# Splitting the first weight load of a decode kernel into four strided loads

## The chip, the cores and the metric

The kernel runs on one core of one Trainium2 chip. The metric is the device time of one execution in microseconds (us), of which the median over several runs is taken. The kernel before takes 692.08 us (three runs, 692.03 to 692.16). A share of 0.2% of that is 1.38 us.

## What is computed

One decode step of a gated mix of attention and a feed-forward block, for one token, all in float32. Cut to what matters:

```python
# x: 1x1x512; k_cache, v_cache: 1x8x32768x128; wq: 512x4096; wo: 4096x512
# w1, w3: 512x1792; w2: 1792x512; gate_w: 512
g = sigmoid((x * gate_w).sum(-1, keepdims=True))
q = (x @ wq).reshape(1, 1, 32, 128).transpose(0, 2, 1, 3)
k, v = repeat(k_cache, 4, axis=1), repeat(v_cache, 4, axis=1)   # 32 query heads on 8 kv heads
p = softmax(einsum("bhqd,bhkd->bhqk", q, k) * 128 ** -0.5)
a = einsum("bhqk,bhkd->bhqd", p, v).transpose(0, 2, 1, 3).reshape(1, 1, 4096) @ wo
b = (silu(x @ w1) * (x @ w3)) @ w2
out = g * a + (1 - g) * b
```

Every weight and every cache row is read once: 296 MB, nearly all of it the two caches (8 heads, 16.8 MB of keys and 16.8 MB of values for each).

## The kernel before, in words

Three regions of SBUF of 128 partitions x 64 KB each (`ra`, `rb`, `rc`) take all the large loads in turn. All of them are issued by SyncE (SP), in an order that the code writes out by hand.

The first three loads stand in `tile_gated_mix_decode_kernel`, ahead of the rest of the program: `wq` into `rc` (line 34 of the loop, semaphore `l_q`), then `w1` and `w3` into the two parts of `rb` (`l_w1`, `l_w3`). `wq` is viewed as 128 rows of 64 KB, one for each partition: four rows of the weight matrix lie in one partition. A jump (L38) with a barrier of all engines follows, since the first part of the program is closed there, and `_program` begins.

In `_program` SP issues the two halves of the first head's first key region (L131, L132, into `ra`), and then every further load waits for the region that it overwrites: `rb` for the feed-forward matmuls (L134, count `c_e`), `ra` and `rb` for the score matmuls (L138, L145, count `c_k`), `rc` for the copies of the query and then for the value matmuls (L143, L147). ScalarE (ACT) issues three small transfers: `x` (L168), `gate_w` (L169) and a row of zeros to the output (L175).

TensorE (PE) turns `x` onto the partitions (L200), makes the sum of the gate (L209), waits for `wq` (L210) and multiplies it (L215, 64 matmul records), then takes `w1` and `w3` (L242). VectorE (DVE) transposes the query rows (L227), ScalarE copies them into place (L231), and the loop over the eight heads starts: VectorE transposes the keys in 32x32 blocks (L355), TensorE makes scores (L284) and multiplies the values of the head before (L298), ScalarE makes the exponentials (L399). After the last head come the output projection with `wo` (L434) and the second feed-forward matrix `w2`, in five pieces (L441, L451).

Of the kernel before, what the change touches and what calls it, by code (L numbers as in the profile page):

```python
# [9 lines left out]
P = 128  # L10
# [14 lines left out]
@with_exitstack  # L25
def kernel(ctx, tc, x, k_cache, v_cache, wq, wo, w1, w3, w2, gate_w, out):
    nc = tc.nc
    rb, rc = (nc.alloc_sbuf_tensor(n, [P, 16384], F32).ap() for n in ("rb", "rc"))
    l_q, l_w1, l_w3 = (nc.alloc_semaphore(n) for n in ("l_q", "l_w1", "l_w3"))
    loads = [(rc, wq, l_q)]  # L30
    n = w1.shape[0] * w1.shape[1] // P
    loads += [(rb[:, i * n:(i + 1) * n], w, sem) for i, (w, sem) in enumerate(((w1, l_w1), (w3, l_w3)))]
    for to, w, sem in loads:
        i = nc.sync.dma_start(to, w.rearrange("(p c) n -> p (c n)", p=P)).then_inc(sem, 16)

        tc.no_tile_sem_insts.add(i.ins.name)
    tc.close()
    tc.compile()  # L38
    _program(nc, rb, rc, l_q, l_w1, l_w3, x, k_cache, v_cache, wq, wo, w1, w3, w2, gate_w, out)


def _program(nc, rb, rc, l_q, l_w1, l_w3, x, k_cache, v_cache, wq, wo, w1, w3, w2, gate_w, out):
    pe, dve, act, pool, sp = nc.tensor, nc.vector, nc.scalar, nc.gpsimd, nc.sync
# [163 lines left out]
    dve.tensor_copy(xp[:, :, 0], mc[:, NC:2 * NC]).then_inc(t_x, 1)  # L207
    take(t_x, 2)
    n_gate = c_q.by(pe.matmul(mc[:, 0:1], ones[0:1], gsm[0:1], start=True, stop=True))  # L209
    pe.wait_ge(l_q, 16)  # L210
    for c in range(NC):
        for b in range(2):
            for j in range(4):
# [225 lines left out]
    for k in range(W2[1]):  # L439
        t = k % 4  # L440
        i = pe.matmul(  # L441
            acc[32 * t:32 * t + 32, :], htp[:, k, :], w2t[:, k, :], start=False, stop=(k >= W2[1] - 4),
            skip_group_check=True,
        )
# [65 lines left out]
```

## Time and profile before

| what | value |
|---|---|
| median of three runs | 692.08 us |
| span of the profiled execution, first to last instruction | 690.5 us |
| what lies around the span, by the median | 1.6 us |
| busy: TensorE, VectorE, ScalarE, GpSimd | 55%, 44%, 6%, 1% of the span |
| mean granted TensorE clock | 0.763 of full speed |
| read from HBM | 296.23 MB, 429 GB/s over the span |
| packets on SP's queue | 6192, 99.3% of 16 DMA engines' span |

How to read it: the share of a compute engine says how long it worked, not whether anybody waited for it. The DMA share is the mean over the core's 16 DMA engines of the time in which a packet of theirs was on its way, so 1.00 is all 16 engines busy all of the time. In a table by windows, the bytes and the time of a packet are counted in the window in which it starts. So in a window shorter than a packet the share can lie far above 1, and such rows tell how many packets started: a packet of `wq` is one row of 65,536 bytes. Packets on SP's queue can be counted from the program: 5504 rows, and for each of the 43 transfers one small packet on each of 16 engines, together 6192.

### The profile page before, as it was taken

Reading aid. Unit: us, or ns where it says so; the run is one execution under the profiler, and the core shown is the slowest. Engines: PE = TensorE matmul, PEld = TensorE weight load, DVE = VectorE, ACT = ScalarE, POOL = GpSimd, SP = SyncE. Lnnn points to the kernel's source line nnn. Section 1 sums busy time; section 2 is a strip of 40 time slices with the busy share of each in tenths; the row PEclk is TensorE's granted clock in tenths of the full one; section 3 lists DMA queues with packets and bytes.
Section 4 is the critical chain, followed back from the end, with each engine's and each line's share of the span. In section 5 each row is a group of like instructions: output and inputs, shape, how many; then the busy total and the mean of one; then the engine's idle time right before and its main releaser. Section 6 shows DMA issues by size and latency. Waiting matters only on the chain. (4 is left out here: it accounts for less than half of the span.)

```text
span 690.5 us, 6710 instructions
## 1 busy us (share of the span) xinstructions
PE 380.2 (55%) x2946; PEld 107.8 (16%) x2946; DVE 307.0 (44%) x194; ACT 41.7 (6%) x111; POOL 7.1 (1%) x41
## 2 busy tenths in 40 slices
PE   1737256466463744567563735457463734466567
PEld 1200011103010121103020211103010211103122
DVE  1019378291725537091725447091815446191000
ACT  0020011002000010002000010002000010002000
POOL 0000000000000000000000000000000000000000
PEclk9975587879685876768577967778676966768678
DMA  9999999999999999999999999999999999999997
GB/s 410 400 434 455 425 430 430 448 440 429 426 429 437 425 437 444 437 429 425 433 433 433 444 440 429 425 429 437 429 444 440 433 425 429 437 425 437 441 417 318
DMA packets 6222, 296.35 MB, mean 429 GB/s; under 512 B 707, under 2 KB 963, under 8 KB 1094
## 3 DMA queue, kind: packets, MB, share of 16 engines
q1 hardware_dynamic: 6192, 296.23, 99.3%
q8 instruction: 6, 0.10, 0.1%
q14 instruction: 2, 0.02, 0.0%
q10 hardware_dynamic: 22, 0.01, 0.0%
HBM read 296.23 MB, written 0.00 MB: 429 GB/s over the span
## 5 line engine op out<-in xcount | busy, mean ns | idle before, releaser
L355 DVE STREAM_TRANSPOSE rb<-rb 128x2048 f32<-128x2048 f32 x64 | 141.8, 2274 | 150.3 <-DVEq L125 150.3
L284 PE MATMUL psum<-rb,winbuf 128*32 128x512 f32 x512 | 96.7, 836 | 122.9 <-PEq L125 122.9
L355 DVE STREAM_TRANSPOSE ra<-ra 128x2048 f32<-128x2048 f32 x64 | 141.4, 2276 | 43.0 <-DVEq L125 43.0
L298 PE MATMUL psum<-rc,prob 128*32 128x512 f32 x896 | 112.8, 660 | 41.3 <-PEq L125 41.3
L284 PE MATMUL psum<-ra,winbuf 128*32 128x512 f32 x512 | 87.5, 782 | 83.8 <-PEq L125 83.8
L298 PEld LDWEIGHTS psum<-rc,prob 128*32 128x32 f32 x896 | 33.6, 121 | 117.0 <-issue 116.8
L379 DVE TENSOR_REDUCE mx<-psum 128x4 f32<-128x1024 f32 x8 | 9.8, 1225 | 82.7 <-DVEq L125 82.7
L284 PEld LDWEIGHTS psum<-rb,winbuf 128*32 128x32 f32 x512 | 13.5, 125 | 202.7 <-issue 202.7
L393 ACT COPY sbuf<-psum 128x512 f32<-128x512 f32 x16 | 9.9, 618 | 478.0 <-PE psum L284 478.0
L284 PEld LDWEIGHTS psum<-ra,winbuf 128*32 128x32 f32 x512 | 14.9, 122 | 149.3 <-issue 149.3
L399 ACT ACTIVATE prob<-psum,nm 128x256 f32<-128x256 f32 x32 | 18.9, 695 | 39.3 <-DVE nm L387 39.3
L308 PE MATMUL psum<-ident,sbuf 128*64 128x64 f32 x512 | 16.7, 223 | 0.8 <-PEq L125 0.8
L308 PEld LDWEIGHTS psum<-ident,sbuf 128*64 128x64 f32 x512 | 15.6, 138 | 7.6 <-issue 7.6
L360 DVE SCALAR_TENSOR_TENSOR otall<-psum,gate,recip 128x4 f32 (+1 forms) x8 | 1.7, 214 | 32.8 <-DVEq L125 32.8
L298 PE MATMUL psum<-rb,prob 128*32 128x512 f32 x64 | 8.5, 690 | 9.7 <-DMA rb<-in_A_v_cache_dram 9.7
L215 PE MATMUL psum<-rc,xp 128*32 128x512 f32 x64 | 9.8, 782 | 4.7 <-DMA rc<-in_A_wq_dram 4.7
L434 PE MATMUL psum<-rc,oq 128*32 128x512 f32 x64 | 10.7, 829 | 2.6 <-DMA rc<-in_A_wo_dram 2.2
L271 POOL COPY winbuf<-winraw 32x16 f32<-32x16 f32 x32 | 6.1, 191 | 535.4 <-PE psum L284 499.7
L242 PE MATMUL psum<-rb,xp 128*32 128x448 f32 x64 | 8.6, 690 | 5.4 <-DMA rb<-in_B_w_dram 5.4
L298 PE MATMUL psum<-ra,prob 128*32 128x512 f32 x64 | 9.6, 770 | 3.3 <-DMA ra<-in_A_v_cache_dram 3.3
L200 PE MATMUL psum<-ones,ob 1*128 1x1 f32 x8 | 2.0, 370 | 15.2 <-DMA prob<-in_gate_w_dram 15.2
L318 PE MATMUL psum<-fold,ob 128*128 128x4 f32 x64 | 8.4, 255 | 0.8 <-PEq L125 0.8
(62 smaller groups left out, 79.0 us busy)
## 6 DMA issues: line engine op xcount, KB each, us to landing
ra<-in_A_k_cache_dram SPq DMA_DIRECT2D x2, 4096.0 KB, 52.6
rc<-in_A_wo_dram SPq DMA_DIRECT2D x2, 4096.0 KB, 45.5
rb<-in_B_w_dram SPq DMA_DIRECT2D x2, 3584.0 KB, 34.7
ra<-in_B_w_dram SPq DMA_DIRECT2D x1, 1792.0 KB, 33.4
ra<-in_B_w_dram SPq DMA_DIRECT2D x1, 1024.0 KB, 35.5
ra<-in_B_w_dram SPq DMA_DIRECT2D x1, 512.0 KB, 36.3
ra<-in_B_w_dram SPq DMA_DIRECT2D x2, 128.0 KB, 36.0
rc<-in_A_v_cache_dram SPq DMA_DIRECT2D x14, 30.4
```

The source lines that it names most:

```text
L215: m = pe.matmul(pq[b][32 * j:32 * j + 32, :], xp[:, c, :], rc[:, o:o + REP * DH], start=(c == 0), stop=(c == NC - 1),)
L242: i = pe.matmul(ps[32 * j:32 * j + 32, 0:FJ], xp[:, c, :], rb[:, o:o + FJ], start=(c == 0), stop=(c == NC - 1))
L271: pool.tensor_copy(winbuf[32 * r:32 * r + 32, 16:144].rearrange("p (c k) -> p c k", k=32)[:, :, 4 * r:4 * r + REP], winraw[32 * r:32 * r + ...
L284: i = pe.matmul(s_ps[m][32 * g:32 * g + 32, :], winbuf[:, w:w + 32], region.rearrange("p (n c i) -> p c n i", c=4, i=32)[:, c, n:n + 16], ...
L298: i = pe.matmul(o_ps[32 * t:32 * t + 32, :], prob[:, w:w + 32], region[:, n * DH:(n + 4) * DH], start=(r == 0 and g == 0 and f == 0), stop ...
L308: i = pe.matmul(pf[64 * s:64 * s + 64, 64 * a:64 * a + 64], sbuf[:, a].rearrange("p i m -> p (i m)"), ident.rearrange("p (gf r s q) -> p s ...
L318: i = pe.matmul(mb[:, 0:REP], ob[:, b * P:(b + 1) * P], fold[:, 4 * b:4 * b + 4], start=(b == 0), stop=(b == 3))
L355: dve.transpose(part[:, c], part[:, c]).then_inc(t_tr, 1)
L379: dve.tensor_reduce(mx, pf.rearrange("p (a q) -> p q a", q=REP), axis=AX.X, op=ALU.max).then_inc(t_mx, 1)
L393: act.copy(sbuf[:, :, :, m], s_ps[m].rearrange("p (n i) -> p n i", i=32)).then_inc(t_ev, 1)
L399: act.activation(prob[:, 0:1024].rearrange("p (a n q) -> p n a q", a=16, q=REP)[:, :, :, q], pf.rearrange("p (n a q) -> p n a q", n=16, q= ...
L434: pe.matmul(acc[32 * t:32 * t + 32, :], oq[:, k:k + 32], rc[:, k * D:(k + 1) * D], start=(k < 4), stop=False, skip_group_check=True,)
```

## The change

The one load of `wq` becomes four loads into the same places, each of some of the partitions: every eighth from 0 (16 rows), every eighth from 4 (16 rows), every fourth from 2 (32 rows), every second from 1 (64 rows). Together they are the 128 rows. All four raise `l_q` by 16, and TensorE waits for 64 in place of 16. Source rows go with the partitions, so each partition holds what it held before.

```diff
-    loads = [(rc, wq, l_q)]
-    n = w1.shape[0] * w1.shape[1] // P
-    loads += [(rb[:, i * n:(i + 1) * n], w, sem) for i, (w, sem) in enumerate(((w1, l_w1), (w3, l_w3)))]
+    wqd, w1d, w3d = (w.rearrange("(p c) n -> p (c n)", p=P) for w in (wq, w1, w3))
+    n = w1d.shape[1]
+    parts = [slice(first, P, step) for first, step in ((0, 8), (4, 8), (2, 4), (1, 2))]
+    loads = [(rc[s], wqd[s], l_q) for s in parts]
+    loads += [(rb[:, 0:n], w1d, l_w1), (rb[:, n:2 * n], w3d, l_w3)]
     for to, w, sem in loads:
-        i = nc.sync.dma_start(to, w.rearrange("(p c) n -> p (c n)", p=P)).then_inc(sem, 16)
+        i = nc.sync.dma_start(to, w).then_inc(sem, 16)
...
-    pe.wait_ge(l_q, 16)
+    pe.wait_ge(l_q, 64)
```

The only engine whose list of instructions changes is SP, at its start. Before, SP's first instructions are these (destination, source, partitions x elements, and in brackets the semaphore that one waits for; "in_B_w" is `w1`, `w3` or `w2`):

```order
L505 UNCONDITIONAL_BRANCH [waits barrier_Pool_Activation_PE_DVE_SP_release]
L34 DMA rc<-in_A_wq_dram 128x16384
L34 DMA rb<-in_B_w_dram 128x7168 x2
L38 UNCONDITIONAL_BRANCH
L131 DMA ra<-in_A_k_cache_dram 128x8192 [waits barrier_Pool_Activation_PE_DVE_SP_release]
L132 DMA ra<-in_A_k_cache_dram 128x8192
L134 DMA rb<-in_A_k_cache_dram 128x16384 [waits c_e]
```

After the change, the same place reads (line numbers are higher by two):

```order
L507 UNCONDITIONAL_BRANCH [waits barrier_Pool_Activation_PE_DVE_SP_release]
L36 DMA rc<-in_A_wq_dram 16x16384 x2
L36 DMA rc<-in_A_wq_dram 32x16384
L36 DMA rc<-in_A_wq_dram 64x16384
L36 DMA rb<-in_B_w_dram 128x7168 x2
L40 UNCONDITIONAL_BRANCH
L133 DMA ra<-in_A_k_cache_dram 128x8192 [waits barrier_Pool_Activation_PE_DVE_SP_release]
L134 DMA ra<-in_A_k_cache_dram 128x8192
L136 DMA rb<-in_A_k_cache_dram 128x16384 [waits c_e]
```

Three more transfers stand ahead of `w1` and `w3`, ahead of the barrier behind the jump (L38, now L40), and so ahead of the first keys; nothing else has moved, on SP or elsewhere.

## The prediction

> **What bounds the kernel now.** I read the page first, then stretches of the span, then the first microseconds.
>
> ```profile
> DMA  9999999999999999999999999999999999999997
> q1 hardware_dynamic: 6192, 296.23, 99.3%
> 22.50:342.50 320.00, 180.25 (x1354) 46.79 (x1354) 164.12 (x97) 21.86 (x61) 3.82 (x20) 0.75 1.00 434
> 342.50:662.50 320.00, 175.20 (x1378) 50.67 (x1382) 138.79 (x85) 16.73 (x44) 2.29 (x12) 0.75 1.00 433
> ```
>
> The page's DMA digits never fall from the first slice to the last but one, and SP's queue fills 99.3% of 16 engines' span. The last two columns of the windows are DMA share and GB/s: 1.00 and 434, then 1.00 and 433, over 640 us in which keys, values, VectorE's share and the clock's ups and downs all differ. The kernel is bound by its transfers, and they run against one flat ceiling. From the queue's row one engine moves 296.23 MB / (16 x 0.993 x 690.5 us) = 27.0 GB/s, so one row of `wq`, 65,536 bytes, takes 2.42 us, and the 8 rows that each engine has of `wq` 19.4 us.
>
> So whatever `wq` gains or loses at the front moves all that stands behind it, unless a cover exists. I looked for one in SP's own waits and in how long the first keys take:
>
> ```profile
> SPq L147 <- PE psum L298: 264.5, 7, 40.5
> SPq L134 <- PE psum L242: 42.8, 1, 42.8
> 3.22 0.43 SPq L132 DMA_DIRECT2D ra<-in_A_k_cache_dram  x1
> 46.50 0.33 SPq L134 DMA_DIRECT2D rb<-in_A_k_cache_dram  x1
> DMA to landing us min/median/max: 57.2/57.2/57.2
> rc<-in_A_v_cache_dram SPq DMA_DIRECT2D x14, 30.4
> ```
>
> SP does wait for buffers, but always with work queued. The second half of the first keys (issued at 3.22, the fifth row is its time to landing) lands at 60.4 us, while the next load is issued at 46.5 us: 14 us of queue are left. In the heads a value load takes 30.4 us from issue to landing, of which its own 128 rows need 19.4: 11 us of queue stand ahead. The engines are therefore never short of work, and both quantities shift with `wq` alike. A delay or gain in front reaches the end one to one; there is no slack in which it could vanish, and none in which it is made up.
>
> The end also hangs on the transfers:
>
> ```profile
> 677.63 2.14 another core or an unknown queue
> 679.82 5.34 PE psum L434 x32
> ```
>
> The second piece is TensorE's work on the second half of `wo`, and the gap before it is the wait for that half to land.
>
> **What the change takes from the start.** Here a gain is possible. Windows of 0.1 us tell when the first rows start (16 engines, one row each; 655 GB/s in 0.1 us is one row, 3277 is five):
>
> ```profile
> 1.70:1.80 0.10, 0.00 (x0) 0.00 (x0) 0.00 (x0) 0.00 (x0) 0.00 (x0) 1.00 9.89 3277
> 3.00:3.10 0.10, 0.00 (x0) 0.00 (x0) 0.08 (x1) 0.00 (x0) 0.05 (x1) 1.00 1.52 655
> 4.70:4.80 0.10, 0.00 (x0) 0.00 (x0) 0.00 (x0) 0.10 (x1) 0.00 (x0) 1.00 1.51 655
> 5.50:5.60 0.10, 0.00 (x0) 0.00 (x0) 0.00 (x0) 0.10 (x1) 0.00 (x0) 1.00 1.51 655
> ```
>
> Five engines start their first row at 1.7 us and the last at 3.0. The second rows start between 4.7 and 5.5, so the early ones needed 3 us for the first row, the last 2.4. The last engine stays 0.8 us behind the first. If the engines start late because descriptors for 128 rows are written before the last engine gets its first one, then a first load of 16 rows, one for each engine, takes away up to 3.0 - 1.7 = 1.3 us, and 0.8 us if the first engine's second row is the best that all can have. If it is a cost of the first access itself, it takes nothing. I take -0.4, the middle of 0 and the observed 0.8, and keep 0 to -1.3.
>
> **What it adds in issues and packets.** Three more transfers are issued by SP:
>
> ```profile
> 0.73 0.37 SPq L34 DMA_DIRECT2D rc<-in_A_wq_dram  x1
> 1.16 0.90 SPq L34 DMA_DIRECT2D rb<-in_B_w_dram  x2
> 2.84 0.33 SPq L131 DMA_DIRECT2D ra<-in_A_k_cache_dram  x1
> 22.84 9.81 PE L215 MATMUL psum<-rc,xp 128*32 128x512 f32 x64 [4.68 <-DMA rc<-in_A_wq_dram]
> 15.23 2.02 PE L200 MATMUL psum<-ones,ob 1*128 1x1 f32 x8 [15.23 <-DMA prob<-in_gate_w_dram]
> 21.60:21.70 0.10, 0.00 (x0) 0.00 (x0) 0.00 (x0) 0.00 (x0) 0.00 (x0) 1.00 0.67 287
> 687.00:688.00 1.00, 1.00 (x41) 0.80 (x36) 0.00 (x0) 0.51 (x1) 0.00 (x0) 1.00 0.35 119
> 688.00:689.00 1.00, 0.90 (x28) 0.59 (x19) 0.24 (x1) 0.24 (x1) 0.00 (x0) 1.00 0.00 0
> ```
>
> At 0.43 to 0.45 us each they push `w1`, `w3`, the barrier and everything issued behind it by 1.3 us. For SP that is covered by the rows of `wq` already queued: the first row of `w1` starts at 21.6 us (287 GB/s in 0.1 us is its 28,672 bytes), and it would be issued at 2.5. The barrier also delays ScalarE's small loads of `x` and `gate_w`, for which TensorE waits until 15.23 us. Behind them stand the gate and `xp`, and then TensorE has 4.68 us to spare before `wq` lands. A shift of 1.3 us, or of one more row of 2.42 us if their packets slip behind one, stays inside. Were that cover gone, TensorE would start L215 later; that costs nothing either until the 14 us of queue at L134 are used up. Cost: 0.
>
> The 3 x 16 more small packets: the engines are idle for 0.7% of 690.5 us, 4.8 us, of which 1.7 lie before the first row and some 2.5 behind the last (the last two rows: none starts after 688). At most 0.6 us are left for 43 transfers, 0.014 each. Three more cost at most 0.05 us.
>
> **What it does to the rate of `wq`.** This is the large unknown. Every large load of before covers 128 neighbouring partitions in one instruction, so whichever engine serves which partition, the pairing has always been the same, and the ceiling of 434 belongs to that pairing. The four parts break it: at one time the 16 engines write 16 partitions that lie 8 apart (part 1), then 16 others (part 2), and in parts 3 and 4 each engine's rows lie 4 and 2 apart. Two readings of the ceiling exist, and no row separates them. If the limit sits in the engine, 8 rows cost 8 x 2.42 us in any order: extra 0. If it sits where the data enters SBUF, with as many entrances as engines, and rows 8 apart fall on half of the entrances, then two engines share one for each row: 4.84 us in place of 2.42, extra 2.42 for each of 8 rows, 19.4 us. Two engines that share an entrance run in step, since they started together and go through the same sequence, so they meet again at the next row. What they are apart at the start, up to 0.8 us by the rows above, is saved on every collision: one collision costs 2.42 us less that distance. But the last pair decides, and among 8 pairs some are closely in step; I take -0.3 for this, and keep 6 x 0.8 = 4.8 us (six rounds, since two neighbouring rows on one entrance save only once) as the bound.
>
> I take the upper end, 19.4. The ceiling is the same for keys and values, for first and last heads, for rows of 64, 32 and 28 KB: the reading side changes addresses and sizes all the time and the rate does not move. What never changes is the set of destination partitions. That leaves engine or entrance, and an entrance that is just as wide as an engine is the natural partner of a flat 27.0 GB/s for each.
>
> [...]
>
> **The sum.** -0.4 (start) + 0.05 (packets) + 19.4 (sharing) - 0.3 (pairs not quite in step) = +18.7 us. Span 690.5 + 18.7 = 709.2 us; with the 1.6 us around it, which the median of 692.08 has beside the span, 710.8 us. Its own range: at most 19.4 + 0.05, at least 19.4 - 4.8 - 1.3 = 13.3, so 705.4 to 711.5.
>
> **Rivals.**
> - *The engine is the limit.* For it: each engine moves 27.0 GB/s whatever it moves. Against it: nothing in this trace. Then only the start counts: 692.08 - 0.4 = 691.7, between 690.7 and 692.1. It decides if a row keeps 2.42 us when its partition is 8 away from its neighbour's. This ends not slower.
> - *Only parts 1 and 2 collide.* If the rows of parts 3 and 4 are dealt out so that an entrance gets one engine at a time, or the pairs fall out of step after the first collisions, two rows cost double: 2 x 2.42 - 0.4 = +4.4, or 696.5, and up to 705 if they fall out of step later.
> - *The split does not place rows as it says.* If engines are tied to partitions, part 1's 16 rows go to 8 engines with two rows each, part 2's to the other 8, and each engine still has 8 rows in all at full rate. The order changes, the sum of rows does not: 692.1, with the start unimproved.
>
> [...]
>
> **How the numbers follow.** Full collisions 0.50, partial 0.17, engine's limit 0.24, rows tied to engines 0.07, a start that gains over 1.38 us 0.02. A measurement of this kernel can tell about 0.2%, 1.38 us, from no change. Slower: 0.50 + 0.17 = 0.67; same: 0.24 + 0.07 = 0.31; faster: 0.02. Leaving out either side would leave out more than 2 in 10, so the range reaches from the engine's limit with a good part of the start's gain, 691.0, to full collisions without any relief, 711.5; the likeliest case's own range stands above.
>
> **What would show it.** In windows of the first 45 us the DMA rate would be near 217 GB/s until about 41 us and 434 behind it, and TensorE's L215 (then L217) would start near 41.5 in place of 22.84. From there every row of the timeline is that of before, 18 to 19 us later: SP's L134 issue near 65 us, and the wait for `wo` the same length. If L215 starts at 22.0 to 22.8, the engine is the limit. If it starts near 27, only two rows collided. If the second rows start at 4.2 us on all engines the start was a matter of descriptors; if the first rows take 3 us again it was not. The prediction is wrong also if the delay shows at L215 and not at the end: then a cover that I deny exists.

## The result, and the profile after

The kernel with the change takes 697.24 us (median of five runs, 697.14 to 697.45) against 692.03 us for the kernel before in the same session: ratio 1.0077, 95% interval 1.0066 to 1.0088, or +5.2 us. The direction was forecast, the size was not: +18.7 us was the forecast, and 697.24 lies 0.7 us above the rival in which only parts 1 and 2 collide.

The page after the change, for the lines shown of before (DMA digits; SP's queue with packets, MB and share):

```profile
span 695.7 us, 6713 instructions
DMA  9999999999999999999999999999999999999997
GB/s 275 418 421 450 427 426 462 426 422 433 426 445 441 426 426 433 437 448 426 426 433 437 448 426 426 433 426 452 433 422 430 430 445 441 426 426 433 434 423 321
q1 hardware_dynamic: 6240, 296.23, 99.3%
```

Before, the rates of the 40 slices were:

```profile
GB/s 410 400 434 455 425 430 430 448 440 429 426 429 437 425 437 444 437 429 425 433 433 433 444 440 429 425 429 437 429 444 440 433 425 429 437 425 437 441 417 318
```

The span grew by 5.2 us. The queue's share is still 99.3%, and the digits look as full as before: the engines count as busy while a row crawls (a share of 1.04 at 223 GB/s, below). Only the rate tells: 275 GB/s in the first of 40 slices in place of 410, and from the second on about what it was. The 48 more packets (6240 for 6192) are the three loads' own.

Windows of the changed kernel show row by row what happened (last two columns DMA share and GB/s; 16 rows of 65,536 bytes start in each of these stretches but the second: 1311 x 0.8, 953 x 1.1, 955 x 1.1, 1751 x 0.6 and 1501 x 0.7 are all 1.05 MB):

```profile
2.00:2.80 0.80, 0.00 (x0) 0.00 (x0) 0.00 (x0) 0.00 (x0) 0.00 (x0) 1.00 6.08 1311
4.00:6.50 2.50, 0.00 (x0) 0.00 (x0) 1.11 (x5) 0.00 (x0) 0.79 (x5) 1.00 0.00 0
6.50:7.60 1.10, 0.00 (x0) 0.00 (x0) 0.03 (x1) 0.68 (x1) 0.00 (x0) 1.00 4.47 953
11.40:12.50 1.10, 0.00 (x0) 0.00 (x0) 0.00 (x0) 0.00 (x0) 0.00 (x0) 1.00 2.65 955
14.60:15.20 0.60, 0.00 (x0) 0.00 (x0) 0.00 (x0) 0.00 (x0) 0.00 (x0) 1.00 4.07 1751
17.00:17.70 0.70, 0.00 (x0) 0.00 (x0) 0.00 (x0) 0.00 (x0) 0.00 (x0) 1.00 3.48 1501
```

The 16 rows of part 1 start between 2.0 and 2.8, those of part 2 between 6.5 and 7.6, the first 16 of part 3 between 11.4 and 12.5, and none between 4.0 and 6.5. Where 16 rows start in a stretch, its length times the DMA share is the mean time of a row: 0.8 x 6.08 = 4.86 us in part 1, 1.1 x 4.47 = 4.92 in part 2, then 2.92, 2.44 and 2.44. The kernel before, with the first two rounds of its `wq`:

```profile
1.70:3.10 1.40, 0.00 (x0) 0.00 (x0) 0.08 (x1) 0.00 (x0) 0.20 (x1) 1.00 2.15 749
4.70:5.60 0.90, 0.00 (x0) 0.00 (x0) 0.00 (x0) 0.90 (x1) 0.00 (x0) 1.00 2.69 1165
```

There the first row took 1.4 x 2.15 = 3.01 us and the second 0.9 x 2.69 = 2.42. In two longer stretches of the changed kernel (parts 1 and 2; parts 3 and 4) and in the two stretches of 320 us that were shown of before:

```profile
2.00:11.40 9.40, 0.00 (x0) 0.00 (x0) 1.14 (x5) 1.28 (x1) 0.79 (x5) 1.00 1.04 223
11.40:26.70 15.30, 2.58 (x10) 2.43 (x10) 1.67 (x4) 0.17 (x1) 0.00 (x0) 1.00 0.98 412
22.50:342.50 320.00, 169.57 (x1338) 46.51 (x1338) 158.90 (x94) 21.83 (x61) 3.79 (x20) 0.77 1.00 432
342.50:662.50 320.00, 174.74 (x1386) 50.48 (x1382) 143.98 (x87) 16.71 (x44) 2.27 (x12) 0.77 1.00 433
```

Half the rate (223 GB/s), with a DMA share of 1.04, for the two rounds of 16 rows; nearly the full rate (412) for the other six rounds; and behind that nothing differs (432 and 433 in place of 434 and 433).

The timeline after the change, and two other rows on SP (the first keys' landing time and its waits):

```profile
0.73 2.48 SPq L36 DMA_DIRECT2D rc<-in_A_wq_dram  x4
5.12 0.33 SPq L133 DMA_DIRECT2D ra<-in_A_k_cache_dram  x1
18.10 2.02 PE L202 MATMUL psum<-ones,ob 1*128 1x1 f32 x8 [18.10 <-DMA prob<-in_gate_w_dram]
27.81 9.50 PE L217 MATMUL psum<-rc,xp 128*32 128x512 f32 x64 [6.79 <-DMA rc<-in_A_wq_dram]
51.10 0.33 SPq L136 DMA_DIRECT2D rb<-in_A_k_cache_dram  x1
DMA to landing us min/median/max: 59.8/59.8/59.8
SPq L149 <- PE psum L300: 264.5, 7, 40.6
```

TensorE starts on `wq` at 27.81 in place of 22.84, +4.97 us. The second half of the first keys (issued at 5.5 us) lands at 65.3 in place of 60.4, +4.9, with the next load issued at 51.1: the 14 us of queue are still there, and SP's long wait at L149 is the 264.5 us that it was at L147. The delay arose in the first three rounds, which end near 15 us, and was carried to the end.

One sign of the prediction did not come: the wait for `wo` is gone. TensorE came to the output projection 6.7 us later (678.99 in place of 672.29) and did both halves in one go; why it came 1.5 us later than the transfers' shift no run shows. The chain that ended last now hangs on the pieces of `w2`, the last transfers of the kernel:

```profile
678.99 9.88 PE L436 MATMUL psum<-rc,oq 128*32 128x512 f32 x64 [0.37 <-PEq L127]
655.87 35.88 DMA ra<-in_B_w_dram
691.79 2.15 PE psum L453 x60
```

The end still waits for a transfer, so the delay reaches it all the same.

### The profile page after: what moved, and what is told of

It is laid out like the page before. It is cut to its first block, busy times and chain, and to the rows that moved or that the text cites. A ratio compares the mean times of both kernels' runs of the same rounds, so it can differ in the third digit from the quotient of the medians.

```text
span 695.7 us, 6713 instructions
## 1 busy us (share of the span) xinstructions
PE 372.4 (54%) x2946; PEld 108.1 (16%) x2946; DVE 307.0 (44%) x194; ACT 41.7 (6%) x111; POOL 7.1 (1%) x41
## 3 DMA queue, kind: packets, MB, share of 16 engines
q1 hardware_dynamic: 6240, 296.23, 99.3%
## 5 line engine op out<-in xcount | busy, mean ns | idle before, releaser
L286 PE MATMUL psum<-rb,winbuf 128*32 128x512 f32 x512 | 92.7, 803 | 126.8 <-PEq L127 126.8
L286 PE MATMUL psum<-ra,winbuf 128*32 128x512 f32 x512 | 82.1, 738 | 88.8 <-PEq L127 88.8
```

The lines of the kernel that those rows point to most:

```text
L286: i = pe.matmul(s_ps[m][32 * g:32 * g + 32, :], winbuf[:, w:w + 32], region.rearrange("p (n c i) -> p c n i", c=4, i=32)[:, c, n:n + 16], ...
```

## The experiments

Three questions were open. Where does a row lose 2.5 us: at the destination (theory S), at the source (H), because a load has only one row for each engine (F), or because the queue has just started (O)? Why did the rows of parts 3 and 4 not lose: are such loads dealt out so that no two engines meet, or did the engines fall out of step (D)? And what became of the start's gain?

### Without loads of 16 rows

```diff
-    parts = [slice(first, P, step) for first, step in ((0, 8), (4, 8), (2, 4), (1, 2))]
+    parts = [slice(first, P, step) for first, step in ((0, 4), (2, 4), (1, 2))]
```

(Here and below, TensorE waits for 16 times the number of loads.) Expected:

> wq in three loads, of 32, 32 and 64 rows (every 4th partition from 0, every 4th from 2, every 2nd from 1); no load of 16 rows is left. Theory S: two engines share one entrance of SBUF where a load's rows crowd, and only loads of 16 rows eight partitions apart do so; then every row of wq takes 2.42 us and the time is that of before, 691.5 to 692.5. Theory H: rows 512 KB apart in HBM come at half rate; loads with rows 256 KB apart are as good as the whole one: 691.5 to 692.5 as well. Theory O: the first two rows on a queue are slow when a load is split, whatever its rows: two rows of 4.9 us, 697. Theory D: the engines do meet in loads of 32 and 64 rows, and fell out of step after the first two collisions: the first rows take 4.9 us here too, 695 to 700.

Measured: 692.27 us against 691.88, ratio 1.0006 (0.9997 to 1.0015). The rate over all of `wq`, then the start of the product:

```profile
2.00:21.90 19.90, 2.58 (x10) 2.44 (x10) 2.82 (x9) 1.46 (x2) 0.79 (x5) 1.00 1.01 422
23.06 9.54 PE L217 MATMUL psum<-rc,xp 128*32 128x512 f32 x64 [4.76 <-DMA rc<-in_A_wq_dram]
```

The whole load, before, from its first row on:

```profile
1.70:21.60 19.90, 2.58 (x10) 2.43 (x10) 2.82 (x9) 1.45 (x2) 0.79 (x5) 1.00 1.00 422
```

The rate is the same, 422 GB/s, so no row is slow. The loss belongs to the loads of 16 rows; O falls for a split as such, and D falls, since engines that begin with 32-row loads would have met there first.

### Eight loads of 16 rows, eight partitions apart

```diff
+    parts = [slice(first, P, 8) for first in (0, 4, 2, 6, 1, 3, 5, 7)]
```

> wq in eight loads of 16 rows, every 8th partition from 0, 4, 2, 6, 1, 3, 5, 7. If every load of 16 rows eight apart is served at half rate (S by the entrances, H by the source, F because a load with one row for each engine is slow), all eight rows take 4.9 us, wq lands near 43 us and the time is 692.0 + 8 x 2.48 - 0.3 = 711.5. Theory D (engines fall out of step after two collisions) and theory O (only the first two rows are slow) expect two or three slow rows: 697 to 700.

Measured: 712.59 us against 691.88, ratio 1.0300 (1.0285 to 1.0316), +20.7 us.

```profile
2.00:41.20 39.20, 2.58 (x10) 2.44 (x10) 2.81 (x9) 1.45 (x2) 0.79 (x5) 1.00 1.01 214
41.20:60.00 18.80, 12.40 (x96) 3.23 (x96) 1.94 (x3) 4.42 (x17) 0.76 (x4) 0.95 1.00 417
```

This is the case that the prediction took the change for: half the rate (214 GB/s) for all eight rows, 39 us long. By D the later rows would be fast again; they are not. The very partitions that went through parts 3 and 4 at 412 GB/s (2, 6, 1, 3, 5, 7 and so on) are slow when they come 16 at a time.

### The same sizes, neighbouring partitions

```diff
+    parts = [slice(0, 16), slice(16, 32), slice(32, 64), slice(64, 128)]
```

> wq in four loads of the same sizes as the change (16, 16, 32, 64 rows), but of neighbouring partitions: 0 to 15, 16 to 31, 32 to 63, 64 to 127. Theory S: neighbouring partitions crowd more. [...] Theory H: source rows 64 KB apart are not 512 KB apart, nothing is slow: 692. Theory F (a load with one row for each engine is slow): two rows of 4.9 us as in the change: 697.

Measured: 721.46 us against 691.88, ratio 1.0428 (1.0412 to 1.0444). The two 16-row loads, the start of each of them, and the loads of 32 and 64:

```profile
1.70:19.30 17.60, 0.00 (x0) 0.00 (x0) 1.14 (x5) 1.28 (x1) 0.79 (x5) 1.00 1.02 119
1.70:2.55 0.85, 0.00 (x0) 0.00 (x0) 0.00 (x0) 0.00 (x0) 0.00 (x0) 1.00 10.11 1234
9.90:11.05 1.15, 0.00 (x0) 0.00 (x0) 0.00 (x0) 0.00 (x0) 0.00 (x0) 1.00 8.20 912
19.30:50.70 31.40, 2.57 (x10) 2.43 (x10) 1.67 (x4) 0.17 (x1) 0.00 (x0) 1.00 0.99 201
```

About a quarter of the whole load's 422 GB/s, then about half. A row of the first load takes 0.85 x 10.11 = 8.6 us, one of the second 1.15 x 8.20 = 9.4. Loads of the same sizes as in the change cost nearly six times as much, so F does not explain the loss: which partitions a load has decides, not how many rows. H does not explain it either, since here the rows of a load are neighbours in HBM.

### Sixteen rows, four apart, in the middle

```diff
+    parts = [slice(32 + j, 96, 4) for j in range(4)] + [slice(0, 32), slice(96, 128)]
```

> wq in six loads: four of 16 rows, every 4th partition from 32, 33, 34, 35 up to 95; then partitions 0 to 31 and 96 to 127, 32 rows each. [...] Theory H (512 KB apart): nothing is slow, 692. Theory O: two slow rows, 697.

Measured: 702.84 us against 691.88, ratio 1.0157 (1.0142 to 1.0173).

```profile
2.00:12.30 10.30, 0.00 (x0) 0.00 (x0) 1.14 (x5) 1.28 (x1) 0.79 (x5) 1.00 1.00 407
12.30:31.70 19.40, 2.58 (x10) 2.43 (x10) 1.67 (x4) 0.17 (x1) 0.00 (x0) 1.00 1.02 216
```

Fast first and slow behind: the 16-row loads at partitions 32 to 95 run at 407 GB/s, nearly the full rate, and the 32-row loads of neighbours at 216, half of it. F, by which the loads with one row for each engine lose, gives the opposite order, so F is out.

### The same sixteen, shifted by 32 partitions

```diff
+    parts = [slice(s + j, s + 64, 4) for s in (0, 64) for j in range(4)]
```

> wq in eight loads of 16 rows with the step of 4 that cost nothing when the loads began at partitions 32 to 35; here they begin at 0 to 3 (up to 63) and at 64 to 67 (up to 127). Count, step and distance of the source rows are the same as there, only the place is shifted by 32 partitions. [...] If the step of 8 itself were slow and not the sharing, every row takes 2.42 us: 692.5.

Measured: 713.03 us against 691.99, ratio 1.0304 (1.0287 to 1.0321).

```profile
2.00:41.30 39.30, 2.57 (x10) 2.43 (x10) 2.82 (x9) 1.46 (x2) 0.79 (x5) 1.00 1.03 214
```

Count, step and distance at the source are those of the fast loads above; only the place differs, and the rate is 214 GB/s in place of 407. The partitions 0, 4, ... 60 crowd, and 32, 36, ... 92 do not.

### Other source rows, same destinations, and the reverse

The change with neighbouring source rows for parts 1 and 2:

```diff
+    sources = [slice(0, 16), slice(16, 32)] + parts[2:]
+    loads = [(rc[s], wqd[f], l_q) for s, f in zip(parts, sources)]
```

> The change with other source rows: parts 1 and 2 go to the same partitions (every 8th), but read rows 0 to 15 and 16 to 31 of the wq view, 64 KB apart in place of 512 KB. It leaves some rows of wq unread and puts others in their place. Theory S (destination): nothing changes, two rows of 4.9 us, 697.2. Theory H (source rows 512 KB apart are slow): all rows 2.42 us, 692.

Measured: 697.14 us against 691.97, ratio 1.0074 (1.0059 to 1.0090).

And source rows 512 KB apart, to destinations that do not crowd:

```diff
+    kr = k_cache.rearrange("a h (r n) d -> (a h r) (n d)", n=P)
+    loads = [(rc[j:P:4], kr[j:256:8], l_q) for j in range(4)]
```

> Four loads of 32 rows, every 4th partition from 0, 1, 2, 3, whose source is the key cache with rows 512 KB apart, in place of wq: it leaves the product with wq's values out. Theory S: 32 rows four apart reach all entrances, every row takes 2.42 us, 692. Theory H: rows 512 KB apart come at half rate: 8 rows of 4.9 us, 711.

Measured: 692.28 us against 691.97, ratio 1.0006 (0.9996 to 1.0015). The first row is of the near source (parts 1 and 2), the second from the other kernel, with the far source (all of its first region):

```profile
2.00:11.40 9.40, 0.00 (x0) 0.00 (x0) 1.14 (x5) 1.28 (x1) 0.79 (x5) 1.00 1.04 223
```

```profile
2.00:21.90 19.90, 2.58 (x10) 2.44 (x10) 2.82 (x9) 1.45 (x2) 0.79 (x5) 1.00 1.01 422
```

The slow rows stay slow with the source near, at the very 223 GB/s of the change, and rows at the full rate keep it with the source far. The source has no part in it: H is out.

### The opposite order

```diff
+    parts = [slice(first, P, step) for first, step in ((1, 2), (2, 4), (4, 8), (0, 8))]
```

> The change's four loads in the opposite order: 64, 32, 16, 16 rows. Theories S and H: the last two rows of each engine take 4.9 us in place of the first two, wq lands where it does in the change, 697.2. Theory O (the start is slow when split): nothing is slow behind the start, 692 if the first loads have more than one row for each engine.

Measured: 697.83 us against 691.97, ratio 1.0083 (1.0068 to 1.0099).

```profile
2.00:17.20 15.20, 1.77 (x8) 1.77 (x8) 2.50 (x7) 1.28 (x1) 0.79 (x5) 1.00 1.00 414
17.20:26.60 9.40, 0.81 (x4) 0.66 (x3) 0.32 (x2) 0.17 (x1) 0.00 (x0) 1.00 1.04 223
```

The slow rows moved to where the 16-row loads stand, so it is no matter of the start. This order took 0.6 us more than the change. The rounds of 16 rows account for it (the first, the two rounds of the 16-row loads and the first rows of `w1`; then the first rows of `w1` in the kernel before):

```profile
2.00:2.80 0.80, 0.00 (x0) 0.00 (x0) 0.00 (x0) 0.00 (x0) 0.00 (x0) 1.00 3.84 1311
17.20:18.00 0.80, 0.45 (x3) 0.40 (x3) 0.17 (x1) 0.00 (x0) 0.00 (x0) 1.00 6.02 1313
21.70:23.05 1.35, 0.00 (x0) 0.00 (x0) 0.00 (x0) 0.00 (x0) 0.00 (x0) 1.00 3.67 777
26.60:28.00 1.40, 0.00 (x0) 0.00 (x0) 0.00 (x0) 0.00 (x0) 0.00 (x0) 1.00 1.19 328
```

```profile
21.60:22.50 0.90, 0.00 (x0) 0.00 (x0) 0.00 (x0) 0.00 (x0) 0.00 (x0) 1.00 1.19 510
```

The slow rows take 4.82 and 4.95 us, 2.4 and 2.5 more than an undisturbed one. In the change the first slow row is also the first row of all, which took 3.01 us before, so that it loses only 1.85 us. Behind the slow rows the first rows of `w1` take 1.4 x 1.19 = 1.67 us in place of 1.07; in the change it is the third round that is longer, by 0.50. Together with the first row of 3.07 that makes 5.6 us here and 4.85 there, 0.7 us apart.

### Two halves

```diff
+    parts = [slice(0, P, 2), slice(1, P, 2)]
```

> wq in two loads of 64 rows, even and odd partitions. Theory S: every row takes 2.42 us and the time is that of before within 0.5 us, 691.6 to 692.5. Theory D (engines meet in loads of 64 rows too when they start in step): slow rows at the start, 695 or more.

Measured: 692.26 us against 691.97, ratio 1.0005 (0.9996 to 1.0014). SP's two issues of `wq` take 1.18 us, the product starts as early as before, and the rate (last line) is that of the whole load:

```profile
0.73 1.18 SPq L36 DMA_DIRECT2D rc<-in_A_wq_dram  x2
3.90 0.33 SPq L133 DMA_DIRECT2D ra<-in_A_k_cache_dram  x1
22.80 9.98 PE L217 MATMUL psum<-rc,xp 128*32 128x512 f32 x64 [6.64 <-DMA rc<-in_A_wq_dram]
2.00:22.00 20.00, 2.58 (x10) 2.43 (x10) 2.82 (x9) 1.46 (x2) 0.78 (x5) 1.00 1.01 420
```

A split that crowds nothing costs nothing that one of these runs can tell from zero, and brings nothing. (All three such splits lie 0.3 to 0.4 us above before, each with an interval that holds 1.) No version of the split was faster than the one load.

## Why the prediction was wrong

**The kernel is bound by its transfers, and what the front loses reaches the end: right.** +4.97 us at the start of the product, +4.9 at the landing of the first keys, +5.2 in span and median. In the runs with +11.0, +20.7 and +29.6 us it held as well (the product started 10.96, 20.49 and 29.51 us later there): no cover swallowed it.

**Where two engines share an entrance a row takes 4.84 us: the size was right, the entrance is not shown.** The slow rows took 4.86 and 4.92 us where 2.42 is the undisturbed row. Of the two readings of the ceiling, the engine alone is out by the destination experiments: loads of 16 rows with the same step give 407 or 214 GB/s by the place of the 16 partitions alone. That the place is an entrance which two engines share remains my reading; no view shows an entrance. The rival in which engines are tied to partitions is out as well: there parts 1 and 2, or the eight loads eight apart, would have filled both halves of the engines, and the time would have stayed at 692.1; measured were 697.24 and 712.59. Every set of partitions in these experiments had one of three rates: 407 to 422 GB/s, 201 to 223, or 119 (0 to 15 and 16 to 31). That there are as many entrances as engines, and that rows 8 apart fall on half of them, no row of before showed; what the runs show is half the rate, 214 GB/s over all eight loads eight apart.

**The step that failed is the number of rows that meet: "extra 2.42 for each of 8 rows, 19.4 us".** I had each engine take rows of parts 3 and 4 that lie 4 and 2 apart, neighbour after neighbour, and so meet another engine on each. No run shows that term of 19.4 us for the change: 2 rows are slow, not 8, and in its place stand 2 x (4.9 - 2.42) = 5.0 us. Loads of 32 and 64 rows with a step of 4 and 2 ran at 422 and 420 GB/s, as the whole load did. How the rows of such a load are dealt to the engines is not shown, since no view names the engine of a row; that they are dealt so that no two engines meet is my inference from the rate. Dealt neighbour after neighbour, as I had it, the engines of part 3 would have begun at partitions 2, 10, ... 122. These are the partitions of the third of the eight loads that ran at 214 GB/s, so the rows would have taken 4.9 us; they took 2.92 and 2.44. In a load of 16 rows all 16 start before the first is done (in part 1 between 2.0 and 2.8 us, of rows that take 4.86), so whichever engine has which row, the same 16 partitions are written at one time. I took one order of dealing for parts 3 and 4 without a row that showed it. The rival that was right, two rows and 696.5, had 0.17 together with all other partial cases.

**That the rows which follow are as slow as the first: right.** In the eight loads of 16, all eight rows were slow (214 GB/s over 39.2 us); of the relief of 0.3 us that I gave to pairs out of step nothing is to be seen: that run took 20.7 us more, where eight full collisions make 19.4.

**The start: -0.4 us was forecast, and it is not there.** Five first rows started at 1.7 us before; with loads that have a step none started before 2.0 (with neighbouring partitions the first started at 1.7 again). The last first row did start sooner: in the halves all 16 started before 2.6 us, where the last one before started at 3.0. But this came to nothing, as the first two rounds of the halves show:

```profile
2.00:2.60 0.60, 0.00 (x0) 0.00 (x0) 0.00 (x0) 0.00 (x0) 0.00 (x0) 1.00 5.23 1748
5.00:5.60 0.60, 0.00 (x0) 0.00 (x0) 0.30 (x2) 0.00 (x0) 0.00 (x0) 1.00 4.04 1748
```

The first rows took 0.6 x 5.23 = 3.14 us, and the second ones started between 5.0 and 5.6, as late as before (4.7 to 5.5). By the prediction's own sign ("if the first rows take 3 us again it was not") the slow start is no matter of descriptors; what it comes from no view shows. SP needed 2.48 us for four issues, 0.62 each, where I had taken 0.43 to 0.45 from the other loads.

**The issues are hidden: right, with a wrong price.** The barrier moved from 2.84 to 5.12 us, 2.3 and not 1.3, and TensorE's first work from 15.23 to 18.10. The cover of 4.68 us would still have held it without the delay of `wq`: with four loads of 32 rows, whose barrier came at 5.07 and TensorE's first work at 15.76, the product started at 23.02, and TensorE waited 4.33 us for its rows even so.

**The sum, and what is left open.** That 2 x 2.48 = 5.0 us comes so near to the 5.2 found is in part luck. By the rounds, the first row lost 1.85 us (4.86 for 3.01), the second 2.50 and the third 0.50, together 4.85; the rest is of the size of the later start of the first rows (0.3 us). The third round starts while the last rows of part 2 are still on their way, which fits its 0.50, but no run separates that. Three runs with slow rows last took more than 2.48 us for each of these: 0.9 us more with the loads eight apart (20.7 for 8 x 2.48 = 19.8), 1.0 with sixteen in the middle (11.0 for 4 x 2.48 = 9.9), 1.2 with the shifted ones (21.0 for 19.8). In the first of them the rows of `w1` behind the slow rows took 1.5 us (1.30 us at a share of 1.14) in place of 1.07, which is 0.4 of it; the rest is open. So are the 0.3 to 0.4 us of the uncrowded splits.

## What to carry to other kernels

For a load into some of the partitions, look at which partitions it has and measure its rate by itself; the number of rows does not give it. In these runs 16 rows at a time ran at 407 GB/s where they lay four apart within 32 to 95, at 214 where they lay four apart within 0 to 63 and 64 to 127, and at 119 as neighbours from 0 to 31. The DMA share read 1.00 to 1.03 in all three, so look at GB/s for the stretch. Splitting a transfer by partitions in this kernel, which is bound by its transfers, was free only where each piece by itself ran at the whole load's rate (420 to 422 GB/s; 692.26 to 692.28 us against 691.88 to 691.97); order and size of the pieces did not make up for it.

## What the runs showed of the hardware

- Loads that do not cover all 128 partitions ran at or near the 422 GB/s of the whole load: four loads of 16 partitions, at 32, 36, ... 92 and the three sets beside it, at 407, and loads of 32 partitions four apart at 422.
- Where partitions crowd, 16 rows ran at a rate that went by their place: 214 GB/s over eight loads like 0, 4, ... 60, and 119 over two loads of 16 neighbours, 0 to 15 and 16 to 31.
- Source rows of 64 KB that lie 512 KB apart in HBM came at 422 GB/s, as the rows of the whole load did, which lie 64 KB apart.
- A load that SP issues to partitions with a step took 0.59 to 0.62 us to issue in these kernels (1.18 for two, 2.48 for four), one to neighbouring partitions 0.49 (1.97 for four), the whole load 0.37.
- A row of 64 KB took 2.42 us undisturbed, 4.82 to 4.95 in the rounds of 16 that crowd in the change and in the opposite order, 5.06 on the mean of the eight shifted ones (39.3 x 1.03 / 8), and 8.6 to 9.4 in loads of 16 neighbours.
